# First softmax rows taken ahead of the visits in a fused attention and feed-forward kernel

## The chip, the cores and the metric

The kernel runs on one core of one Trainium2 chip. The metric is the device time of one execution in microseconds; the median of the runs is compared. Besides that time there is one profiled execution with a trace of every instruction. The engines are called PE (matrix products), PEld (its weight loads), DVE (VectorE), ACT (ScalarE), POOL (GpSimd) and SP (which issues most of the DMAs).

## The reference

Two blocks follow each other. The first is an attention with 32 inducing rows, in two steps; the second a feed-forward layer with a leaky activation whose slope `alpha` belongs to each hidden unit.

```python
# x: (4, 12480, 128), inducing: (32, 128)
def mab(q, kv):
    s = scale * (q @ kv.transpose(0, 2, 1))
    s = s - s.max(-1, keepdims=True)
    a = np.exp(s)
    a /= a.sum(-1, keepdims=True) + 1e-09
    return a @ kv
h = mab(I, x)          # 32 rows look at all rows of a batch
y = mab(x, h)          # every row looks at the 32 rows
# the feed-forward layer: d_model 128, d_ff 2048
u = y @ w_in
g = np.maximum(u, 0.0) + alpha * np.minimum(u, 0.0)
out = g @ w_out
```

Inputs and output are float32; the kernel multiplies in bfloat16.

## The kernel before

The rows of a batch are cut into six super-tiles of 16 tiles of 128 rows, and a short rest of one and a half tiles; the rests of the four batches are done together at the end. The kernel first works through the whole first attention step of batch 0 (the start). Then come the visits. One visit takes a block of four tiles (512 rows) and four of the 16 slices of the hidden units: PE makes four products `hh` of 32x512 operands (line 808, in `visit`), each into a PSUM bank of its own; DVE or ACT applies the relu and writes `gt` (lines 823 and 821); in the visit after, PE makes 16 products of `gt` and the weights `W1` (line 834, in `second`) that are summed in the block's bank `bp`. So a block takes four visits, a super-tile 16, and the whole 390. PSUM has eight banks, and they are shared by everything.

The value `y` is never made: `HW` is the product of the 32 rows `h` and `w_in`, so the softmax weights of a row, turned into the operand `a2`, give `hh` directly. The leaky part is linear: with `Amat`, the product of `w_in` and the alpha-weighted `w_out` (`linear_product`, line 996), `a_lin` makes `HA` (lines 619 and 621), and `linear` adds it for two blocks at a time (line 861). For the first pair of blocks this is put off to visit 8, where `finish` for the first block is put off too.

The softmax weights of a super-tile take several steps: scores on PE (`b_products`, line 644) and their copy (`b_scores`, line 702 or 704), maximum (line 721, DVE), subtraction (line 726, POOL), exponential (line 688, ACT), sum (line 712, POOL), reciprocal (`b_rec`, line 749, DVE), multiplication (line 757, POOL) and the turn by a transposing DMA (`b_turn`, line 766). For the first super-tile this takes too long, so it has a way of its own: maximum, subtraction and exponential without copy (lines 675, 679 and 773), the turn of tiles 0 to 7 by PE and a copy (lines 779 and 787), that of tiles 8 to 15 by a POOL copy and a DMA (`first_turn_dma`, lines 1144 and 1147); the division by the sum comes at the end of the block, by the reciprocal `rec` (`first_sum`, line 1154 on POOL; `first_rec`, line 1167 on DVE; used in line 880). The scores of tiles 4 to 15 wait in the eighth bank (`later`).

The order of the instructions is written out by hand. In the start it is the string `order`, whose words are carried out by `begin`; `W5` is five products without use. In the visits every step is put at a visit with `at(n, step, ..., cost=...)`; it is issued at the end of that visit, behind the visit's own relus on each engine. A table `when` holds the visits of the eight steps of a super-tile. A planner (`Plan.choose`) looks at all visits with assumed costs ahead of time and chooses, by a beam search, which engine does each relu and copy, which bank is used, and whether a step runs at once or in the middle of the visit after. It begins with a state: when PE, ACT and DVE are free, and when each bank is. Steps on POOL and DMAs have no cost in it.

```python
start = tuple(self.NEVER if k == BANKS - 1 else 0.0 for k in range(BANKS))
beam = [((0.0, 0.0, 0.0, (0.0,) * R, start, (), ()), None)]
```

The end of `order`, and the steps of the ramp that follow it:

```python
W4 b bm b2 bs be w hwv W5 bt ba W5
...
at(6, first_rec, cost=[("v", 160)])
at(6, linear_product, cost=[("s", 900), ("v", 210), ("!", 0)])
at(7, a_lin, st, cost=[("s", 260), ("v", 210)])
```

Of the kernel before, what the change touches and what calls it, by code (L numbers as in the profile page):

```python
# [21 lines left out]
P = 128  # L22
R = 4
ST = 16
BT = 4
# [5 lines left out]
def kernel(  # L31
# [80 lines left out]
    class Plan:  # L112
# [115 lines left out]
            return (*new, tuple(held.items()), tuple(waits)), used  # L228

        def choose(self):  # L230
            start = tuple(self.NEVER if k == BANKS - 1 else 0.0 for k in range(BANKS))
            beam = [((0.0, 0.0, 0.0, (0.0,) * R, start, (), ()), None)]
            relus = ["".join(w) for w in product("av", repeat=R) if 0 < w.count("a") < R]
            for n, (*_, chains) in enumerate(self.visits):
                ways = []
                for chain in chains:
                    kinds = [k for k, _ in chain]
                    if "f" in kinds:
                        ways.append([e + w for e in "av" for w in "nl"])
                    elif "!" in kinds or not {"a", "v"} & set(kinds):  # L240
                        ways.append([""])
                    else:
                        ways.append(["n", "l"])
                found = {}
                for state, path in beam:
                    for way in product(*ways):
                        for relu in relus:
                            new, used = self.step(state, n, relu, way)
                            at = new[0] + 390
                            over = max(new[1] - at, 0) + max(new[2] - at, 0)  # L250
                            over += sum(w[1] for w in new[6]) * 0.3
                            score = new[0] + 0.3 * over
                            ends = sorted(max(x - new[0], -200) for x in new[4])
                            key = (
                                *(int(x - new[0]) // 16 for x in new[1:3] + new[3]),
                                *(int(x) // 16 for x in ends if x < self.NEVER / 2),
                                new[6],
                            )
                            if key not in found or score < found[key][0]:
                                found[key] = (score, new, (path, relu + "".join(way), used))  # L260
                best = sorted(found.values(), key=lambda f: f[0])[: self.WIDTH]
                beam = [(new, path) for _, new, path in best]
            path, taken, banks = beam[0][1], [], []
            while path:
                path, these, used = path
                taken.append(these)
                banks.append(used)
            self.taken = iter("".join(reversed(taken)))
            self.banks = iter([k for used in reversed(banks) for k in used])
# [405 lines left out]
        nc.vector.tensor_reduce(out=m[:, :n], in_=ps[:, t0 : t0 + n, :], axis=AX, op=MAX)  # L675
        return m

    def b_less(ps, t0, n, m, e):
        nc.vector.tensor_tensor(
            out=e[:, :n],  # L680
            in0=ps[:, t0 : t0 + n, :],
            in1=m[:, :n].unsqueeze(2).broadcast_to([P, n, M]),
            op=SUB,
        )

# [6 lines left out]
    def new_e():  # L692
        return e2_pool.tile([P, ST, M], f32, name="e2", tag="e2")
# [77 lines left out]
    def b_exp_once(e, n, w):  # L771

        nc.scalar.activation(out=w, in_=e[:, :n], func=EXP, scale=scale)
# [235 lines left out]
    def first_most():  # L1009
        kept["bm"] = b_most(kept["b"], 0, BT)  # L1010

    def first_less():
        kept["be"] = new_e()
        b_less(kept["b"], 0, BT, kept["bm"], kept["be"])
# [23 lines left out]
    def begin(step):  # L1038


        if step[0] == "W":
            warm(int(step[1:]))
            return
        plain = {
            "mg": lambda: a_max(st),
            "rb": lambda: kept.update(rb=a_factors_pe(st)),
            "mm": lambda: a_factors_min(st, kept["rb"]),
            "mf": lambda: a_factors_exp(st),
            "ex": lambda: a_worth(st),
            "dn": lambda: a_total(st),  # L1050
            "pd": lambda: kept.update(pd=a_den_pe(st)),
            "rec": lambda: a_den_rec(st, kept["pd"]),
            "ph": lambda: kept.update(ph=a_sum_pe(st)),
            "hT": lambda: a_sum_div(st, kept["ph"]),
            "b": first_products,
            "bm": first_most,
            "bs": first_less,
            "be": lambda: b_exp_once(kept["be"], BT, w0[:, :BT]),
            "bt": lambda: kept.update(bt=b_turn_pe(w0[:, :BT], BT)),
            "ba": lambda: b_turn_copy(st, 0, 0, BT, kept["bt"], False),  # L1060
            "b2": lambda: b_products(st, 0, BT, ST - BT, later),
            "w": lambda: a_w(st),
            "al": lambda: kept.update(al=alpha_turn()),
            "alc": lambda: nc.vector.tensor_copy(out=alT[:], in_=kept["al"][:]),
            "kwp": lambda: nc.gpsimd.tensor_copy(out=w_in_b[:], in_=kept["w_in"][:]),
            "om": lambda: nc.gpsimd.tensor_scalar(
                out=om_al[:], in0=alT[:], scalar1=-1.0, scalar2=1.0, op0=MULT, op1=ADD
            ),
            "hw": lambda: a_w_copy(st),
            "hwv": lambda: a_w_copy(st, False),  # L1070
        }
        if step in plain:
            plain[step]()
            return
        f, act = step[0], step[-1] == "a"
        p, _, part = step[1:].rstrip("avp").partition(".")
        pc = first_pieces[int(p)]
        if f in "tc":
            t0, n = cuts[pc.n][int(part)]
            if f == "t":  # L1080
                kept["t", p, part] = a_turn_pe(st, pc, t0, n)
            else:
                a_turn_copy(st, pc, t0, n, kept.pop(("t", p, part)), act)
        elif f == "k":
            a_cast_part(st, pc, *cuts[pc.n][int(part)], step[-1])
            done = first_pieces[int(p)].s
            if pc.full and step == last_cast[done]:
                load_next(done)
            if step == weights_after:
                load_weights()  # L1090
        elif f == "u":
            kept["u", p] = a_e1_pe(st, pc)
        elif f == "v":
            a_e1_copy(st, pc, kept.pop(("u", p)), act)
        else:
            {"s": a_scores, "m": a_least, "e": a_exp, "f": a_fac, "h": a_h, "g": a_add}[f](st, pc)
# [13 lines left out]
        c5.1a e4 k7.0p f4 om kwp t6.1 c5.2v c5.0v W2 t6.0 c6.1v s5 t7.1 u3 c6.0v t7.0 m5  # L1110
        c7.0v s6 u4 f3 c7.1a m6 v3a W1 h3 e5 v4v e6 s7 f5 m7 W2 u5 mg f6 h4 v5v g3 u6 e7
        ex f7 g4 W1 h5 rb v6v u7 g5 v7a h6 mm mf dn g6 W2 h7 g7 pd rec W1 ph hT W4 b bm
        b2 bs be w hwv W5 bt ba W5
    """
    waiting = [first_pieces[5:6], first_pieces[6:]]
    last_cast = {}
# [4 lines left out]
    for step in order.split():  # L1121
        begin(step)
        if step == "kwp":
# [2 lines left out]
                weights(i, nc.gpsimd)  # L1126
            for i in range(NV):
                linear_weights(i)
    e2s = {}

    def first_rest_less(t0, n):
        e2s[t0] = new_e()
        b_less(later, t0, n, b_most(later, t0, n), e2s[t0])

    def first_rest_exp(t0, n):
        b_exp_once(e2s[t0], n, w0[:, t0 : t0 + n])

    def first_turn():
        act = plan.on_act()
# [59 lines left out]

        todo.setdefault(max(n, 0), []).append((fn, args, cost))  # L1200

    at(0, first_rest_less, BT, BT, cost=[("v", 600), ("!", 0)])
    at(1, first_rest_exp, BT, BT, cost=[("a", 330), ("!", 0)])
    at(1, first_rest_less, H, H, cost=[("v", 780), ("free", BANKS - 1), ("!", 0)])
    at(2, first_turn, cost=[("s", 350), ("f", 0)])
    at(2, first_rest_exp, H, H, cost=[("a", 560), ("!", 0)])
    at(2, first_turn_dma)
    at(6, first_rec, cost=[("v", 160)])
    at(6, linear_product, cost=[("s", 900), ("v", 210), ("!", 0)])
    at(7, a_lin, st, cost=[("s", 260), ("v", 210)])  # L1210
    blocks[0].later = True

    def on(b, fn, *args):
# [2 lines left out]
    for b, s, nt in groups[1:]:  # L1216
        n = first[b, s]
        when = [n - 23, n - 19, n - 16, n - 14, n - 13, n - 11, n - 9, n - 6]
        if (b, s) == (0, 1):
            when = [1, 2, 3, 4, 5, 7, 8, 8]  # L1220
        if (b, s) == (0, 2):
            when[7] = n - 7
        at(when[0], on, b, b_scores, s, nt, cost=[("s", 25 * nt), ("f", 0)])
        at(when[1], on, b, b_max, s, nt, cost=[("v", 70 + 33 * nt)])
        at(when[2], on, b, b_less_pool, s, nt)
        at(
            when[3],
            lambda b=b, s=s, nt=nt: b_exp(states[b].e2[s], nt),
            cost=[("a", 100 + 27 * nt)],
        )  # L1230
        at(when[4], on, b, b_sum, s, nt)
        at(when[5], on, b, b_rec, s, nt, cost=[("v", 160)])
        at(when[6], on, b, b_mul, s, nt)
        at(when[7], on, b, b_turn, s, 0, nt)
# [130 lines left out]
```

## Time and profile before

| | |
|---|---|
| median of 3 runs | 594.98 us (593.67 to 595.17) |
| the profiled execution | 593.7 us |
| its span in the trace | 591.9 us |
| mean granted clock of TensorE | 0.998 |
| start, up to the first `hh` of visit 0 | 30.03 us |
| instructions | 23144 |

The span runs from the first to the last instruction of the trace; some 1.8 us of the execution lie outside it. All times of single instructions below are counted from the start of the span. A row of the timeline gives start, length, engine, line, operation, what is written and read, how many instructions were merged, and in brackets the idle time of the engine before it and what ended it. In the chain of waits a row is a start, a length and what the chain went through.

### The profile page before, as it was taken

What the parts mean: (1) busy time and instruction counts of PE and PEld (TensorE: products, weight loads), DVE (VectorE), ACT (ScalarE), POOL (GpSimd) and SP (SyncE); (2) the same over time, 40 slices, a digit from 0 to 9 for tenths busy, and PEclk for the clock granted to TensorE, in tenths of its full rate; (3) what the DMA queues carried; (4) which work ended last, traced back from release to release, by engine and by line L of the source; (5) the groups of instructions that cost most, each with busy time, mean ns of one, the idle gap of its engine ahead of it and who ended that gap; (6) DMA issues with size and microseconds to landing.
All of it is one profiled execution on the core that took longest, in us unless ns stands there. A gap on an engine that the chain in (4) does not pass through costs nothing.

```text
span 591.9 us, 23144 instructions
## 1 busy us (share of the span) xinstructions
PE 584.5 (99%) x9500; PEld 441.3 (75%) x9500; DVE 535.5 (90%) x978; ACT 537.3 (91%) x1086; POOL 216.6 (37%) x260
## 2 busy tenths in 40 slices
PE   9999999999999999999999999999999999999997
PEld 6667777777777777777777777777777777777776
DVE  5889999999999898999999899999999999989996
ACT  5698999999999999999999999999999998999986
POOL 3494633323326426313226256124034034144010
PEclk9999999999999999999999999999999999999999
DMA  8969999233187999631368999731321331532421
GB/s 338 265 180 167 250 207 225 62 90 91 38 237 161 209 193 211 127 82 60 86 151 180 190 249 207 144 100 38 92 72 55 92 75 53 119 81 61 91 69 47
DMA packets 122347, 80.56 MB, mean 136 GB/s; under 512 B 103760, under 2 KB 106112, under 8 KB 119168
## 3 DMA queue, kind: packets, MB, share of 16 engines
q1 hardware_dynamic: 122016, 78.99, 56.3%
q8 instruction: 74, 1.21, 0.9%
q14 instruction: 33, 0.27, 0.2%
q10 hardware_dynamic: 224, 0.09, 0.1%
HBM read 28.07 MB, written 25.56 MB: 91 GB/s over the span
## 4 chain that ended last, share of the span: by engine, by line
PE 91%; DMA 5%; POOL 2%; DVE 0%; issue 0%; DVEq 0%; SPq 0%; ACT 0%; POOLq 0%
PE bp L834 64%; PE hh L808 21%; DMA xs<-in_x_dram 3%; PE bp L861 2%; DMA w_out_f<-in_moe_w_out_dram 2%; PE hh L644 2%; PE hh L473 1%; PE hh L379 1%; DMA e<-e1T 1%; POOL W L977 1%; POOL AW L986 1%; POOL t L712 0%; DVE gt L823 0%; DVEq L1360 0%; DVE xn L349 0%
## 5 line engine op out<-in xcount | busy, mean ns | idle before, releaser
L821 ACT ACTIVATE gt<-hh 128x512 bf16<-128x512 f32 x854 | 454.8, 605 | 36.0 <-PE hh L808 30.9
L823 DVE TENSOR_SCALAR gt<-hh 128x512 bf16<-128x512 f32 x706 | 453.5, 684 | 23.8 <-PE hh L808 13.3
L834 PE MATMUL bp<-W,gt 128*128 128x128 bf16 x6240 | 417.3, 220 | 0.2 <-DVE gt L823 0.2
L834 PEld LDWEIGHTS <-gt 128*128 128x128 bf16 x6240 | 349.4, 98 | 84.9 <-issue 76.6
L808 PE MATMUL hh<-a,HW 32*128 32x512 bf16 (+2 forms) x1664 | 156.2, 371 | 0.5 <-ACT gt L821 0.5
L757 POOL TENSOR_TENSOR rep<-e,rc 128x2048 bf16<-128x2048 f32 (+1 forms) x24 | 84.5, 3520 | 23.9 <-DVE rc L749 23.5
L726 POOL TENSOR_TENSOR e<-e,smx 128x512 f32<-128x512 f32 (+1 forms) x24 | 24.6, 1025 | 156.4 <-ACT gt L821 89.6
L808 PEld LDWEIGHTS <-HW 32*128 32x128 bf16 x1664 | 40.6, 91 | 41.7 <-issue 5.6
L712 POOL TENSOR_TENSOR t<-e 128x256 f32<-128x256 f32 (+1 forms) x24 | 17.2, 717 | 139.8 <-ACT e L688 139.7
L887 ACT COPY ob<-bp 128x512 f32<-128x512 f32 (+1 forms) x62 | 36.3, 585 | 4.3 <-PE bp L834 1.4
L712 POOL TENSOR_TENSOR t<-t 128x128 f32<-128x128 f32 (+3 forms) x100 | 30.3, 303 | 7.8
L330 POOL CAST xn<-xs 128x2048 bf16<-128x2048 f32 x17 | 32.1, 1888 | 2.8 <-DMA xs<-in_x_dram 2.3
L889 DVE COPY ob<-bp 128x512 f32<-128x512 f32 x32 | 22.0, 687 | 6.0 <-PE bp L834 6.0
L861 PEld LDWEIGHTS <-a 32*128 32x128 bf16 x392 | 15.0, 93 | 6.3 <-issue 0.5
L393 DVE TENSOR_SCALAR_CACHE_REDUCE s<-hh 128x512 f32<-128x512 f32 (+2 forms) x29 | 18.0, 619 | 1.6 <-PE hh L379 1.6
L861 PE MATMUL bp<-HA,a 32*128 32x128 bf16 x392 | 19.1, 214 | 0.2 <-DVE HA L621 0.2
L418 ACT ACTIVATE e1T<-s,rm 128x512 bf16<-128x512 f32 (+1 forms) x25 | 17.9, 718 | 0.6 <-DVE rm L402 0.6
L721 DVE TENSOR_REDUCE smx<-e 128x16 f32<-128x512 f32 (+1 forms) x24 | 15.9, 662 | 0.0
L963 PE MATMUL bp<-blank 128*128 128x256 bf16 x78 | 14.0, 316 | 1.2 <-DVE blank L909 1.2
L688 ACT ACTIVATE e<-e 128x512 f32<-128x512 f32 (+1 forms) x24 | 15.0, 625 | 0.2 <-POOL e L726 0.2
L489 DVE SCALAR_TENSOR_TENSOR hs<-hs,fac,hh 128x128 f32<-128x128 f32 (+1 forms) x25 | 8.6, 344 | 6.4 <-PE hh L473 5.7
L702 ACT COPY e<-hh 128x512 f32<-128x512 f32 (+1 forms) x23 | 13.9, 606 | 0.2
(110 smaller groups left out, 203.7 us busy)
## 6 DMA issues: line engine op xcount, KB each, us to landing
out_dram<-ob SPq DMA_DIRECT2D x97, 256.0 KB, 2.7
xs<-in_x_dram SPq DMA_DIRECT2D x23, 1024.0 KB, 6.6
xs<-in_x_dram SPq DMA_DIRECT2D x2, 512.0 KB, 9.1
w_in_f<-in_moe_w_in_dram SPq DMA_DIRECT2D x1, 1024.0 KB, 4.8
a<-rep SPq DMA_TRANSPOSE x25, 4.7
xT<-xn SPq DMA_TRANSPOSE x18, 6.0
e<-e1T SPq DMA_TRANSPOSE x18, 3.8
xs_left<-in_x_dram SPq DMA_DIRECT2D x4, 64.0 KB, 5.2
```

Source lines behind the costliest of these rows:

```text
L330: nc.gpsimd.tensor_copy(out=st.xn[s][:], in_=xs[:])
L393: nc.vector.tensor_scalar(out=s1[:parts, :cols], in0=ps[:parts, :cols], scalar1=-scale, scalar2=None, op0=MULT, op1=MIN, accum_out=st.mx[: ...
L712: nc.gpsimd.tensor_tensor(out=t[:, :n], in0=src[:, :n, :w], in1=src[:, :n, w : 2 * w], op=ADD)
L726: nc.gpsimd.tensor_tensor(out=st.e2[s][:, :n], in0=st.e2[s][:, :n], in1=st.m2[s][:, :n].unsqueeze(2).broadcast_to([P, n, M]), op=SUB,)
L757: nc.gpsimd.tensor_tensor(out=rep[:, :n], in0=st.e2[s][:, :n].unsqueeze(2).broadcast_to([P, n, R, M]), in1=rc[:, :n].unsqueeze(2).unsqueez ...
L808: nc.tensor.matmul(hh[:, q * cols + w.start : q * cols + w.stop], HWs[b][rows, v * P : (v + 1) * P], a2[rows, t0 : t0 + nt, :].rearrange(" ...
L821: nc.scalar.activation(out=gt[:, :cols], in_=hh[:, :cols], func=RELU)
L823: nc.vector.tensor_relu(gt[:, :cols], hh[:, :cols])
L834: nc.tensor.matmul(blk.acc[:, t * C : (t + 1) * C], gt[:, (q * nt + t) * P : (q * nt + t + 1) * P], W1[:, k, :], start=(not blk.begun), st ...
L861: nc.tensor.matmul(blk.acc[w, t * C : (t + 1) * C], blk.a2[rows, blk.t0 + t, w], HAs[b][rows, :], start=(not blk.begun and t == 0), stop=F ...
L887: nc.scalar.copy(out=ob[:, :nt], in_=acc)
L889: nc.vector.tensor_copy(out=ob[:, :nt], in_=acc)
```

## The change

The maximum of tiles 4 to 15 of the first super-tile is taken in one instruction ahead of the visits (`rx`), and so are the subtractions of tiles 4 to 7 (`rl`) and 8 to 15 (`rk`) and the exponential of tiles 4 to 7 (`re`). The cast of `HW` in the start goes from DVE (`hwv`) to ACT (`hw`). The turn of tiles 4 to 7 (`first_turn`) goes from visit 2 to visit 0, and the scores of the second super-tile from visit 1 to visit 0. In the ramp `linear_product` goes from visit 6 to 5, `a_lin` from 7 to 6, and the reciprocal of the second super-tile (`b_rec`) from 7 to 8. The planner begins with the eighth bank free at 430 ns and DVE free at 330 ns.

```diff
-            start = tuple(self.NEVER if k == BANKS - 1 else 0.0 for k in range(BANKS))
-            beam = [((0.0, 0.0, 0.0, (0.0,) * R, start, (), ()), None)]
+            start = tuple(430.0 if k == BANKS - 1 else 0.0 for k in range(BANKS))
+            beam = [((0.0, 0.0, 330.0, (0.0,) * R, start, (), ()), None)]
...
-    def b_less(ps, t0, n, m, e):
+    def b_less(ps, t0, n, m, e, a=0):
         nc.vector.tensor_tensor(
-            out=e[:, :n],
+            out=e[:, a : a + n],
             in0=ps[:, t0 : t0 + n, :],
-            in1=m[:, :n].unsqueeze(2).broadcast_to([P, n, M]),
+            in1=m[:, a : a + n].unsqueeze(2).broadcast_to([P, n, M]),
             op=SUB,
         )
...
+    def rest_most():
+        kept["rm"] = b_most(later, BT, ST - BT)
+        kept["re"] = new_e()
+
+    def rest_less(t0, n):
+        b_less(later, t0, n, kept["rm"], kept["re"], t0 - BT)
+
+    def rest_exp(t0, n):
+        b_exp_once(kept["re"][:, t0 - BT :], n, w0[:, t0 : t0 + n])
...
+            "rx": rest_most,
+            "rl": lambda: rest_less(BT, BT),
+            "rk": lambda: rest_less(H, H),
+            "re": lambda: rest_exp(BT, BT),
...
-        b2 bs be w hwv W5 bt ba W5
+        b2 bs be w rx hw rl W5 re bt ba rk W5
...
-    at(0, first_rest_less, BT, BT, cost=[("v", 600), ("!", 0)])
-    at(1, first_rest_exp, BT, BT, cost=[("a", 330), ("!", 0)])
-    at(1, first_rest_less, H, H, cost=[("v", 780), ("free", BANKS - 1), ("!", 0)])
-    at(2, first_turn, cost=[("s", 350), ("f", 0)])
-    at(2, first_rest_exp, H, H, cost=[("a", 560), ("!", 0)])
+    at(2, rest_exp, H, H, cost=[("a", 560), ("!", 0)])
+    at(0, first_turn, cost=[("s", 350), ("f", 0)])
     at(2, first_turn_dma)
     at(6, first_rec, cost=[("v", 160)])
-    at(6, linear_product, cost=[("s", 900), ("v", 210), ("!", 0)])
-    at(7, a_lin, st, cost=[("s", 260), ("v", 210)])
+    at(5, linear_product, cost=[("s", 900), ("v", 210), ("!", 0)])
+    at(6, a_lin, st, cost=[("s", 260), ("v", 210)])
...
         if (b, s) == (0, 1):
-            when = [1, 2, 3, 4, 5, 7, 8, 8]
+            when = [0, 2, 3, 4, 5, 8, 8, 8]
```

More of the change, by code (lines that the diff above doesn't have):

```diff
@@ L1128 @@
                 linear_weights(i)
[L1129 to L1136, printed above, removed]
     def first_turn():
```

## The prediction

> **What bounds the kernel now.** I read four views, in this order: the page, the chain of waits over the first 60 us, the timeline of the ramp (24 to 54 us), and the starts of single visits in that timeline. On the page TensorE is the engine that never rests:
>
> ```profile
> PE 584.5 (99%) x9500; PEld 441.3 (75%) x9500; DVE 535.5 (90%) x978; ACT 537.3 (91%) x1086; POOL 216.6 (37%) x260
> ```
>
> So time can be won only where PE waits. The chain of waits says where that is: after the loads and the weights it runs through POOL and DVE until 43.2 us, and from there on it is PE's own work.
>
> ```profile
> 33.07 3.99 POOL AW L986 x4
> ...
> 41.16 0.22 POOL den L1154
> 41.38 0.02 issue
> 41.40 0.04 DVE rec L1167
> 41.44 0.13 issue
> 41.57 0.23 DVE Amat L999
> 41.80 1.19 DVE gt L823 x2
> 42.99 0.21 DVE HA L621
> ```
>
> The timeline shows the starts of the visits (the four L808 matmuls) and what stands between them. A plain visit in the steady part takes 1.33 us:
>
> ```profile
> 50.79 0.40 PE L808 MATMUL hh<-a,HW 32*128 32x512 bf16 x4
> 52.12 0.39 PE L808 MATMUL hh<-a,HW 32*128 32x512 bf16 x4
> ```
>
> The ramp, before and after visit 0 starts at 30.03:
>
> ```profile
> 28.51 0.69 DVE L607 CAST HW<-hh 128x512 bf16<-128x512 f32 x1
> 28.51 0.31 ACT L773 ACTIVATE rep<-e 128x128 bf16<-128x128 f32 x1 [2.39 <-DVE e L679]
> 29.49 0.42 DVE L787 COPY a<-hh 128x512 bf16<-128x512 bf16 x1 [0.30 <-PE hh L779]
> ...
> 30.03 0.61 PE L808 MATMUL hh<-a,HW 32*128 32x512 bf16 x7
> 31.13 0.37 PE L808 MATMUL hh<-a,HW 32*128 32x512 bf16 x1 [0.49 <-ACT gt L821]
> 31.43 0.91 PEld L834 LDWEIGHTS <-gt 128*128 128x128 bf16 x16 [1.19 <-DVE smx L675]
> 32.78 0.41 DVE L675 TENSOR_REDUCE smx<-bp 128x8 f32<-128x256 f32 x1
> 33.29 0.42 DVE L679 TENSOR_TENSOR e<-bp,smx 128x256 f32<-128x256 f32 x1
> ```
>
> Three idle stretches of PE follow.
> Fill: visit 0 starts at 30.03, visit 4 at 35.87, so 5.84. The work in it is four times 0.33 (L808) plus three times 1.00 (L834, one visit behind), plus 0.39 for the scores of the second super-tile and 0.39 for the turn (a visit with scores runs from 91.60 to 93.32, one with a turn from 32.83 to 34.55, both 1.72 against 1.33): 5.10. Idle 0.74. The eighth L808 waits at 31.13 for a PSUM bank, and L834 behind it for the first relu outputs and an eighth and ninth bank.
> Visit 8: 42.24 to 44.57 is 2.33; another visit with the L861 products, 49.24 to 50.79, is 1.55. Idle 0.78: L861 waits for HA (42.91 to 43.19), which on DVE stands behind two relus, Amat and the reciprocal L1167, which waits for POOL's L1154 (ready 41.38).
> Visit 9: 44.57 to 46.59 is 2.02, against 1.72 with scores. Idle 0.30: the fourth L808 waits for a bank, because DVE stood 0.86 in front of
>
> ```profile
> 44.05 0.25 DVE L749 RECIPROCAL rc<-den 128x16 f32<-128x16 f32 x1 [0.86 <-POOL den L736]
> ```
>
> In all 1.82 us. After that little is left: in the PE rows 278 plain visits are never under 1.325 and add up to only 2.6 us above that, ramp excluded, in crumbs.
>
> **Part by part.** *Ahead of the visits, DVE.* It gains one maximum over 12 tiles and two subtractions (128x128, 128x256), and loses the HW cast. From L675 at 0.28 (128 columns) and 0.41 (256) the maximum of 384 columns is about 0.54 (an estimate; ends 0.41 and 0.69, those two rows alone and together). From 28.51: maximum to 29.05, subtraction of 0.29 to about 29.45, and L787 cannot start before 29.49 anyway, because PE's transposes end then. So visit 0 stays at 30.03; at the upper end it comes 0.1 late, and nothing makes it earlier. The last subtraction (0.42) runs 29.92 to 30.35, while the first relu could not start before 30.45. Cover: 0.1 us; if gone, the first DVE relu slips by that much.
> *ACT.* HW cast after the first exp, from 28.83. L605, the same cast of the later batches on ACT, takes 0.592; DVE's took 0.692. HW is ready at 29.42, 0.6 before it is used. The exp of four tiles (0.34) follows and ends at 29.8, before its turn is issued at 30.36. Cost nothing, under ACT's idle 1.66 before 30.48. [...]
> *Removed from visits 0 to 2:* on DVE 0.28+0.29+0.41+0.42 = 1.40, on ACT 0.34. No moved step issues a DMA; POOL's order and SP's queue keep theirs.
> *Scores and turn in visit 0.* After four L808 (30.36) PE does the turn and the scores, 0.78, to 31.14: work that fills the wait instead of following it. Banks: four for visit 0, one for each of the two, four for visit 1, one for the sum: eleven of eight, k7 included from 30.4 on. The first two relus end at 31.08 to 31.13, just as visit 1 needs its third bank; the next two at 31.6 to 31.75, so L834 starts at about 31.70. Two copies (0.42 turn, 0.6 scores) now stand among the relus and cost visit 2 about 0.1 on its fourth bank. Then 31.70+1.00+0.33+0.10+1.00+0.33+1.00 puts visit 4 at 35.46 instead of 35.87: gain 0.41. Ends: 0.74 (no idle), and a loss of 0.3 if both copies stand ahead of visit 1's relus on one engine.
> *Amat product in visit 5, HA in visit 6.* The L996 product (0.90 of PE) needs AW, done at 37.07; visit 5's turn for it comes at about 38.0. Amat is then off the reciprocal's back. HA stays behind L1167, which still waits until 41.40; queued behind that on DVE are HA and visit 7's relus, and PE waits for both. HA ends at about 41.85, visit 7's two DVE relus at 43.1, visit 8 starts at 41.83. Its L861 would run at 42.05, its L834 to 43.45 at the earliest; short banks (visit 7's not yet free) make that 43.8. Against 44.57: 0.77, so 0.36 beyond the fill. Ends 0.78 and 0.
> *Second reciprocal from visit 7 to 8.* DVE no longer stands 0.86 in front of L749; it passes it after both L880. Visit 9's 0.30 goes to about 0.15: gain 0.15, ends 0.30 and 0. What is late next: the multiplication on POOL behind it (rival below).
> *Three numbers of the planner* cost no time themselves, but all 390 visits are planned anew. The 2.6 us of crumbs may go up or down; I take 0 with 0.8 either way.
> Sum: 0.41+0.36+0.15 = 0.92 us won (ends 1.82 won, 0.3 lost). The profiled execution took 593.7 with a span of 591.9; it should come to 592.8. The median shown is 594.98, 1.28 above it: 594.1.
>
> **Rivals.**
> A, the whole idle time goes (1.82), perhaps with fewer crumbs: 593.2 down to 592.6. For it: the relu engines are relieved of 1.74 us exactly there. Against it: L1154 on POOL does not move, and DVE reaches it earlier than before. So does ACT its exp L688, which cannot start before 38.95; it idled 0.24 there and would idle some 0.8.
> B, slower: visit 16 waits for its operand. From L749 at 44.05 the operand needs 0.39, 3.61 on POOL, and 4.3 from DMA issue (48.07) to landing: 52.4, i.e. L749 plus 8.35. Visit 16 began at 54.77 and would now at 53.9. With L749 behind two L880 and a relu I expect it at 45.1 to 45.9, landing at 53.5 to 54.3: just on time. From 45.5 on every delay is paid; past 46.4 the gain is gone; at 47.5, behind two more relus, the kernel comes to 596.1, at 48.2 to 596.8.
> C, slower: the planner charges nothing for POOL, so it hands relus of visits 5 to 8 to an engine that in fact stands before POOL. Four badly placed relus at 0.6 to 0.7 with crumbs grown: 596.5 to 597.
> [...]
>
> **The numbers.** A measurement of this kernel tells 0.3%, 1.8 us, from no change: under 593.2 counts as faster, over 596.8 as slower. My forecast, 594.1 (own range 593.3 to 595.2, the ends of the sum with part of the crumbs): 0.50. A: 0.27. B: 0.11, C: 0.09, D: 0.03. I count B and C whole as slower, since their far ends lie there, and D as no change. Faster 0.27, same 0.53, slower 0.20. The range runs from A's lower end, 592.6, to 596.6, near the far end of B and inside C, leaving out some 0.2.
>
> **What would show it.** In the profile after: visit 0 still at 30.0; L779's second group and L644 between the first and the second four L808; L834 first at about 31.7, with no idle over 0.3; visit 4 near 35.5; L996 before visit 6; L1167 still at 41.4, with DVE idle before it; L861 of visit 8 by 42.7; visit 9 near 43.8; L749 at 45 to 46, and no wait of PE at visit 16. The forecast is wrong if visit 0 moves, if visit 9 starts after 44.4, if visit 16 waits for the DMA, or if plain visits average over 1.34.

## The result and the profile after

The changed kernel is slower: 596.56 us median (595.12 to 598.6, 12 runs) against 593.70 (592.79 to 595.17, 12 runs), a ratio of 1.0047 (95% interval 1.0035 to 1.0059). The profiled execution took 597.49, its span is 595.6, 3.7 more than before's. The time lies just inside the range; the sign was forecast wrongly, and more than half of the chances went to no change. That the time lies inside is luck: the forecast was counted from a median of three runs, 594.98, which the twelve runs put at 593.70, and the top end of the range came from two rivals.

The page: PE works 1.3 us longer than before (584.5), and the span has grown by more.

```profile
PE 585.8 (98%) x9500; PEld 442.1 (74%) x9500; DVE 535.9 (90%) x978; ACT 537.4 (90%) x1085; POOL 216.7 (36%) x260
```

The ramp in the timeline after; these rows answer to those shown of before:

```profile
28.75 0.57 ACT L605 CAST HW<-hh 128x512 bf16<-128x512 f32 x1
29.52 0.42 DVE L787 COPY a<-hh 128x512 bf16<-128x512 bf16 x1 [0.23 <-PE hh L779]
29.86 0.41 DVE L679 TENSOR_TENSOR e<-bp,smx 128x256 f32<-128x256 f32 x1
30.05 0.40 PE L808 MATMUL hh<-a,HW 32*128 32x512 bf16 x4
30.38 0.41 PE L779 MATMUL hh<-ident,rep 128*32 128x128 bf16 x16
30.72 0.56 PE L644 MATMUL hh<-hT,xT 128*128 128x32 bf16 x16
31.61 0.90 PEld L834 LDWEIGHTS <-gt 128*128 128x128 bf16 x16 [0.30 <-ACT gt L821]
...
40.62 0.28 DVE L621 CAST HA<-hh 128x128 bf16<-128x128 f32 x1
40.98 0.25 DVE L1173 RECIPROCAL rec<-den 128x16 f32<-128x16 f32 x1
44.05 0.39 PE L808 MATMUL hh<-a,HW 32*128 32x512 bf16 x4
44.20 0.24 DVE L749 RECIPROCAL rc<-den 128x16 f32<-128x16 f32 x1
44.36 1.22 DVE L880 TENSOR_TENSOR ob<-bp,rec 128x512 f32<-128x512 f32 x2
44.58 3.61 POOL L757 TENSOR_TENSOR rep<-e,rc 128x2048 bf16<-128x2048 f32 x1 [0.99 <-PE hh L808]
```

The ramp did what it was to do: visit 0 at 30.05, turn and scores in the gap, visit 9 at 44.05. Counting the first L808 of each visit, visit 10 starts 0.82 us earlier than before, and this lead stays the same to 0.01 us until visit 31. There it ends. The chain of waits now has, at 74 us, a DMA that before's chain does not have, and the waits of PE and the timeline name it:

```profile
74.25 6.42 DMA a<-rep
```

```profile
PE hh L808 <- DMA a<-rep: 3.1, 1, 3.1
```

```profile
80.72 0.50 PE L808 MATMUL hh<-a,HW 32*128 32x512 bf16 x4 [3.09 <-DMA a<-rep]
```

Before, the same visit starts without a wait:

```profile
78.39 0.40 PE L808 MATMUL hh<-a,HW 32*128 32x512 bf16 x4
```

Visit 32 is the first of the third super-tile; its operand is turned by the DMA of L766. From visit 31 to 32 it takes 4.48 instead of 1.33. The restart costs 0.92 more in visit 32 and 0.31 up to visit 36; DVE and ACT had been idle for 3.1 and 3.0 us when it began, and from 80.9 to 84.3 the granted clock of TensorE was 0.50, against 1.00 just before and after: the 16 L834 of visit 32 took 1.89 there, 1.07 in a plain visit. From there the distance hardly moves. So the account of the spans is -0.82 (ramp) + 3.15 + 0.92 + 0.31 + 0.14 (all visits after 36) = 3.7.

Why the turn came late is seen in part on SP's queue, here before and after:

```profile
48.07 1.78 SPq L766 DMA_TRANSPOSE a<-rep  x1
49.95 1.56 SPq L894 DMA_DIRECT2D out_dram<-ob  x2
51.61 1.17 SPq L356 DMA_TRANSPOSE xT<-xn_left  x1
52.88 3.13 SPq L356 DMA_TRANSPOSE xT<-xn  x1
56.06 0.57 SPq L315 DMA_DIRECT2D xs<-in_x_dram  x1
...
66.28 3.00 SPq L356 DMA_TRANSPOSE xT<-xn  x1
...
72.93 2.31 SPq L766 DMA_TRANSPOSE a<-rep  x1
```

```profile
48.22 1.78 SPq L766 DMA_TRANSPOSE a<-rep  x1
50.10 1.57 SPq L894 DMA_DIRECT2D out_dram<-ob  x2
51.76 2.37 SPq L356 DMA_TRANSPOSE xT<-xn_left  x1
54.22 3.26 SPq L356 DMA_TRANSPOSE xT<-xn  x1
57.53 0.97 SPq L315 DMA_DIRECT2D xs<-in_x_dram  x1
...
66.53 4.00 SPq L356 DMA_TRANSPOSE xT<-xn  x1
...
74.25 3.11 SPq L766 DMA_TRANSPOSE a<-rep  x1
```

The second super-tile's turn (the first row) is issued 0.15 later, although PE is 0.82 ahead. Then the first two outputs, issued from 50.1 on, take 5.1 and 4.6 us to land instead of 3.0 and 2.7. The issue of L356 behind them holds the queue for 2.37 instead of 1.17, and the next two rows slip by 1.3 and 1.5. Some issues at 62 to 64 us are early again, with PE; but POOL's cast waits 1.96 for the load `xs`, the turn of L356 behind it holds the queue for 4.00 instead of 3.00, and from 70 us on all are 1.3 late.

```profile
64.61 1.89 POOL L330 CAST xn<-xs 128x2048 bf16<-128x2048 f32 x1 [1.96 <-DMA xs<-in_x_dram]
```

The third turn is issued at 74.25, 1.32 later, takes 6.42 instead of 5.37 and lands at 80.68. Before, it landed at 78.30, and visit 32 began at 78.39: there was 0.09 us to spare, and a lead of PE that the turn does not share would have been lost there.

The stretches view of 53.5 to 56 us (columns: busy time of PE, PEld, DVE, ACT and POOL with counts, clock, DMA share of 16 engines, GB/s), first after, then before, shows that the DMA engines then did almost nothing, with outputs and turns outstanding:

```profile
53.50:56.00 2.50, 2.50 (x41) 1.84 (x39) 2.46 (x5) 2.02 (x5) 0.00 (x0) 1.00 0.18 32
```

```profile
53.50:56.00 2.50, 2.50 (x41) 1.93 (x40) 2.43 (x5) 2.10 (x5) 0.47 (x1) 1.00 1.01 74
```

Among the trace's packets are loads of the program itself, in the queues that the page calls "instruction": 16 KB (q8) and 8 KB (q14) each. In the changed kernel one of q8 began at 51.99 and took 1.76, one of q14 at 53.62 and took 2.23, amid the outputs; before they began at 53.48 and 54.08, when the outputs had all but landed, and took 1.14 and 0.63. The DMA view of 49 to 56 us has one of each, their time as a share of 16 engines; first after, then before:

```profile
q14 instruction: 1, 0.01, 2.0%
q8 instruction: 1, 0.02, 1.6%
```

```profile
q8 instruction: 1, 0.02, 1.0%
q14 instruction: 1, 0.01, 0.6%
```

### The profile page after: what moved, and what is told of

Same layout as the page of the kernel before. It is cut to its first block, busy times and chain, and to the rows that moved or that the text cites. A ratio compares the mean times of both kernels' runs of the same rounds, so it can differ in the third digit from the quotient of the medians.

```text
span 595.6 us, 23148 instructions
## 1 busy us (share of the span) xinstructions
PE 585.8 (98%) x9500; PEld 442.1 (74%) x9500; DVE 535.9 (90%) x978; ACT 537.4 (90%) x1085; POOL 216.7 (36%) x260
## 4 chain that ended last, share of the span: by engine, by line
PE 94%; DMA 4%; DVE 1%; ACT 0%; issue 0%; DVEq 0%; POOL 0%; SPq 0%
PE bp L834 64%; PE hh L808 21%; DMA xs<-in_x_dram 3%; PE bp L861 2%; PE hh L644 2%; PE hh L473 1%; DMA a<-rep 1%; PE hh L379 1%; DVE gt L823 1%; PE bp L963 1%; PE hh L364 0%; PE hh L598 0%; PE hh L456 0%; DVEq L1363 0%; DVE xn L349 0%
## 5 line engine op out<-in xcount | busy, mean ns | idle before, releaser
L834 PE MATMUL bp<-W,gt 128*128 128x128 bf16 x6240 | 418.1, 220 | 0.2 <-DVE gt L823 0.2
L834 PEld LDWEIGHTS <-gt 128*128 128x128 bf16 x6240 | 350.4, 98 | 84.7 <-issue 77.2
L808 PE MATMUL hh<-a,HW 32*128 32x512 bf16 (+2 forms) x1664 | 156.8, 371 | 3.2 <-DMA a<-rep 3.1
L757 POOL TENSOR_TENSOR rep<-e,rc 128x2048 bf16<-128x2048 f32 (+1 forms) x24 | 84.5, 3521 | 24.4 <-DVE rc L749 23.4
L808 PEld LDWEIGHTS <-HW 32*128 32x128 bf16 x1664 | 40.5, 91 | 45.2 <-issue 6.3
```

The lines of the kernel that those rows point to most:

```text
L757: nc.gpsimd.tensor_tensor(out=rep[:, :n], in0=st.e2[s][:, :n].unsqueeze(2).broadcast_to([P, n, R, M]), in1=rc[:, :n].unsqueeze(2).unsqueez ...
L808: nc.tensor.matmul(hh[:, q * cols + w.start : q * cols + w.stop], HWs[b][rows, v * P : (v + 1) * P], a2[rows, t0 : t0 + nt, :].rearrange(" ...
L834: nc.tensor.matmul(blk.acc[:, t * C : (t + 1) * C], gt[:, (q * nt + t) * P : (q * nt + t + 1) * P], W1[:, k, :], start=(not blk.begun), st ...
```

## The experiments

My theory after this was in two parts. "Landing": the lead is real, but it ran into a transfer that had no time to spare. "Program loads": the extra lateness comes from loads of PE's program that the change put among the first outputs. The rivals were the reciprocal's new place, and a worse plan for all visits. The kernels before and after are called B and A. Each ratio is to runs of B made beside that kernel; their medians go from 593.18 to 593.74, so two kernels are compared by their ratios. All distances below are the starts of the first L808 in the traces.

**a_rec7**: A with the reciprocal back at its place.

```diff
-            when = [0, 2, 3, 4, 5, 8, 8, 8]
+            when = [0, 2, 3, 4, 5, 7, 8, 8]
```

> The changed kernel with the reciprocal of the second super-tile back at visit 7. Theory 'landing': PE's lead of 0.82 us is real, but the operand of the third super-tile (visit 32) landed only 0.1 us before its use in the kernel before, and SP's queue behind the second super-tile's turn did not get earlier; then an earlier reciprocal (43.7 instead of 44.2) moves that turn and all behind it up by 0.5, PE loses 0.3 of its lead, and a wait of 1.5 to 2.5 stays at visit 32: 595 to 596. Rival 'reciprocal': the move to visit 8 alone made the operand late; then the wait at visit 32 is gone and the time is 592.9 to 593.3. Rival 'program loads' (transfers at 50 us collide with PE's program loads): wait as in the changed kernel, about 3, 596.5.

593.79, ratio 1.0007 (0.9995 to 1.0019). Nothing waits at visit 32: the operand lands at 77.68, visit 32 starts at 78.07. Both parts of my theory had forecast a wait here, of 1.5 to 2.5 and of about 3, and were wrong in that. But visit 10 is 16.09 after visit 0 instead of 15.72. So the move to visit 8 is worth 0.4 in the ramp, over twice the 0.15 that I gave it, and is at the same time what leads to the loss: it holds back the second turn (47.68 here, 48.22 in A), while it lets PE run ahead. So the rival "reciprocal" is half right; why the landing moves by 3.0 us it does not say.

**a_turn23** and **b_turn23**: the third turn two visits earlier on SP's queue, in A and in B.

```diff
         if (b, s) == (0, 2):
-            when[7] = n - 7
+            when[7] = n - 9
```

> The changed kernel with the turn of the third super-tile issued at visit 23 instead of 25, that is ahead of one other transposing DMA and an output on SP's queue. 'Landing' and 'program loads' alike: issued at about 71.9 instead of 74.25, landing near 78.2, wait at visit 32 0.9 or less, time 594 to 594.4. If the loss were spread over the new plan's visits instead: no change, 596.5.

594.18, 1.0010 (1.0001 to 1.0020): by the ratios 2.2 us better than A. The turn lands at 75.95 and visit 32 does not wait. Some of it comes back between visits 36 and 50, 2.2 us in the trace, with new waits for DMAs:

```profile
PE hh L473 <- DMA e<-e1T: 1.3, 1, 1.3
...
PE hh L808 <- DMA a<-rep: 0.8, 1, 0.8
```

The outputs were slow here as well (3.5 and 5.4); that the queue stayed late for this reason, and the next in it paid, is a reading that no run isolates. A worse plan for the visits is not the cause of A's loss.

> The kernel before with the same move of the turn from visit 25 to 23. 'Landing': nothing waited there, so no gain: within 0.3 us of the kernel before, and the operand lands some 2 us ahead of visit 32. If the kernel before lost time there in runs that were not profiled: faster by up to 0.5.

593.72, 1.0005 (0.9995 to 1.0014), as expected no gain: the operand lands at 74.81, three us ahead, and nobody needs that in B.

**a_phase** and **b_shift24**: more PE instructions at the very start, in the same PE time, so that the loads of PE's program fall elsewhere. In A the load at 52.0 goes away from the outputs, in B the load at 53.5 goes onto them. The helper `warm` gets a second argument, the number of columns.

```diff
-    warm(17)
+    warm(51, 85)    # a_phase, both places; b_shift24: warm(29, 150)
```

> The changed kernel with the two opening blocks of 17 products of 256 columns without use made into 51 of 85 columns each: about the same PE time, but 136 more PE instructions ahead of everything, half of the distance between two loads of PE's program, so that these loads fall at other places. 'Program loads': the first outputs take about 3 us instead of 5.1, the operand lands near 78.3, the wait at visit 32 falls to about 0.8, time 593.8 to 594.4. 'Landing' without any part of the program loads: unchanged, wait 3, 596.5.

593.45, 1.0001 (0.9992 to 1.0009): by the ratios 2.7 us better than A, with an edit that touches no visit. The load comes at 47.87, the next at 57.09; the outputs take 2.6 and 2.5; the third turn is issued at 71.37, the operand lands at 77.67, and of the wait 0.2 is left:

```profile
PE hh L808 <- DMA a<-rep: 0.2, 1, 0.2
```

> The kernel before, with the two opening blocks of 17 products without use as 29 of 150 columns each: the same PE time, 48 more PE instructions, so that the load of PE's program that fell at 53.5 us falls at about 51.9, onto the first outputs, as in the changed kernel; nothing else is changed. 'Program loads': the first outputs take 4.5 us or more instead of 3.0, the operand of the third super-tile lands at 79.5 to 80.7, PE waits 1 to 2.3 at visit 32, time 594.5 to 596. 'Landing' without program loads (the changed kernel's own order makes the transfers late): no change, 593.4.

594.19, 1.0014 (1.0003 to 1.0025): 0.8 slower than B by the ratio, less than expected. The load comes at 51.32, 2.1 after the first output's issue; the outputs take 4.5 and 4.9, the operand lands at 79.09, earlier than expected, and B has A's wait:

```profile
PE hh L808 <- DMA a<-rep: 1.4, 1, 1.4
```

So the place of the program loads makes transfers late or lets them land in time, both ways shown: the first output took 5.13 in A and 2.6 in a_phase, 2.96 in B and 4.5 in b_shift24. But the way from there to visit 32 is not one and the same. In b_shift24 the slow outputs did not make the queue late: the third turn was issued 42.76 after visit 0, against 42.90 in B. It took 6.51 to land instead of 5.37, and another load of PE's program began at 76.70, while it was under way. A has such a load too, at 77.26, and this is the other part of its lateness (1.05, beside 1.32 at the issue); a_phase has one at 73.44 (6.30), and its gain is all in the issue. My theory had only the loads among the outputs. That slow outputs make the queue late is supported by a_phase, where both go away together, and not by b_shift24.

In the traces of A, of B and of their parts, without a shift, the outputs are fast or slow mostly by where PE's load falls behind the first output's issue. A star marks a load of PE's program that began between the third turn's issue and its landing:

| kernel | load after the issue, us | first two outputs took | third turn took | landed | visit 32 began |
|---|---|---|---|---|---|
| B | 3.53 | 2.96, 2.66 | 5.37 | 78.30 | 78.39 |
| a_fill (below) | 3.86 | 2.97, 2.69 | 5.29 | 77.90 | 78.22 |
| a_lin67 (below) | 3.63 | 2.96, 4.31 | 5.33 | 78.62 | 78.79 |
| b_turn23 | 3.51 | 2.96, 2.67 | 4.67 | 74.81 | 77.86 |
| a_rec7 | 3.39 | 2.92, 4.27 | 5.05 | 77.68 | 78.07 |
| before_again (below) | 3.29 | 2.92, 4.20 | 5.37 | 77.39 | 77.72 |
| a_turn23 | 2.97 | 3.48, 5.42 | 5.75* | 75.95 | 76.97 |
| A | 1.89 | 5.13, 4.60 | 6.42* | 80.68 | 80.72 |
| b_places (below) | 1.82 | 4.83, 4.31 | 6.28* | 80.55 | 80.60 |

With the load at 2 us after the issue both outputs are slow; at 3.3 to 3.9 the first is fast, and the second, issued some 1.2 later, either way. In all 15 traces the third turn took 5.75 to 6.51 where a load began within it, and 4.67 to 5.37 elsewhere. The loads follow PE: 136 more of its instructions moved the one at 51.99 to 47.87. The outputs follow POOL and SP: in A L757 ends at 48.19, the second turn is issued at 48.22 and the first output behind it at 50.10. A lead of PE and a delay of the second turn both shift the one against the other; the change made both, 0.82 and 0.15.

**before_again, a_lin67, a_fill, b_places**: what the lead consists of. `before_again` is B once more. `a_lin67` puts the Amat product and HA back to visits 6 and 7; `a_fill` the reciprocal too, so that only the softmax part is left; `b_places` is B with these three places alone.

```diff
+    at(6, linear_product, ...)     # a_lin67, a_fill; b_places: 5
+    at(7, a_lin, st, ...)          # a_lin67, a_fill; b_places: 6
+            when = [0, 2, 3, 4, 5, 7, 8, 8]   # a_fill; b_places: [1, 2, 3, 4, 5, 8, 8, 8]
```

> The kernel before, unchanged, for a second trace. If the start of POOL's weight products (29.04 in the first trace, when w_out landed at 28.90; 28.6 in the changed kernel's) sets L1154 and with it visits 8 and 9, visit 10 comes up to 0.5 earlier where w_out lands at 28.4, and the lead of the changed kernel is 0.3, not 0.82. If visit 10 is at 46.6 again with an earlier landing, the lead is the change's own.

> The changed kernel with the Amat product back at visit 6 and HA at 7; only the ramp is read. By the sum of the prediction this gives back 0.36 of the lead by visit 10, more if DVE's wait for L1154 stands in front of Amat again (up to 0.8). If only POOL's L1154 counts: no change by visit 10.

> The changed kernel with the Amat product back at visit 6, HA at 7 and the reciprocal at 7: only the softmax steps, the turn and the scores are moved. By the prediction's sum visit 4 stays 0.4 to 0.6 earlier after visit 0 than in the kernel before (5.85) and visit 10 too (16.1 there with w_out at 28.4). If POOL's L1154 holds visits 8 to 10 whatever came before: visit 4 at 5.25, visit 10 at 16.1 or later, no gain.

> The kernel before with the three places alone (Amat product at 5, HA at 6, reciprocal at 8). By the sum: visit 4 as before (5.85), visit 10 0.4 to 0.5 earlier, 15.6. If the places help only where the ramp is ahead already: 16.0.

One trace each, so the visits are compared, not the times (592.76, 594.57, 593.49, 595.61). All in us after visit 0, with the end of `den`, POOL's first sum of softmax weights (L1154, or its line in the other kernels), which follows the landing of w_out; the last column is the distance from `den` to visit 10:

| kernel | den | visit 4 | visit 10 | visit 10 after den |
|---|---|---|---|---|
| B, first trace | 11.34 | 5.85 | 16.57 | 5.22 |
| before_again | 11.05 | 5.85 | 16.27 | 5.22 |
| b_turn23 | 10.81 | 5.85 | 16.02 | 5.22 |
| a_lin67 | 10.89 | 5.26 | 16.92 | 6.03 |
| a_rec7 | 10.88 | 5.21 | 16.09 | 5.22 |
| b_places | 10.86 | 5.85 | 15.68 | 4.82 |
| A | 10.89 | 5.21 | 15.72 | 4.83 |
| a_fill | 9.83 | 5.25 | 15.86 | 6.03 |
| b_phase_turn23 (below) | 9.61 | 5.85 | 15.80 | 6.19 |
| a_phase_turn23 (below) | 9.87 | 5.21 | 14.91 | 5.05 |

Three things follow. While `den` ends 10.8 or more after visit 0, visit 10 keeps a fixed distance to it, 5.22 in B and 4.83 in A, and my trace of B had a late one (w_out landed at 28.90; in the others of B at 27.6 to 28.4): with equal `den` the lead is 0.39 and not 0.82. The softmax part wins 0.6 by visit 4 and has lost it again by visit 10: `b_places` without it is as early as A, and `a_rec7`, with it and with Amat and HA, is level with B. And a part alone can do harm: `a_lin67` comes 0.8 later behind `den` than B and gives back 1.2 of A's lead, more than the 0.8 that I had as the most; `a_fill` has the same 6.03, though its `den` is early. `b_places` also has A's wait at visit 32 (80.60), so that the three places, not the softmax part, brought it.

**a_phase_turn23, b_phase_turn23, a_split_phase_turn23, b_split_phase_turn23**: A and B without a wait at visit 32 (both edits above), and with w_out loaded in four parts, so that POOL can begin on the first.

```diff
-        nc.sync.dma_start(out=kept["w_out"][:], in_=...)
+        for i in range(NV):
+            ks = slice(i * R, (i + 1) * R)
+            nc.sync.dma_start(out=kept["w_out"][:, ks, :], in_=...[:, ks, :])
```

> The changed kernel with shifted program loads (51 of 85) and with the third super-tile's turn at visit 23. Both theories: operand lands near 75, no wait at visit 32. If the lead of the ramp is a gain of the change itself: 0.7 to 0.9 under the kernel before, 592.5 to 592.7. If most of the lead came from an earlier landing of w_out in the profiled run: 593.0 to 593.3.

> The kernel before with the shifted program loads and the third turn at visit 23, so that neither kernel waits at visit 32; beside the changed kernel treated alike (593.0, ratio 0.9996 to the kernel before) this gives the change's own worth. If the ramp's lead is the change's: 0.4 to 0.7 slower than that one, 593.4 to 593.7. If new plan and DMA luck are all: the same, 593.0.

Both came to a ratio of 0.9996, with intervals of 0.9985 to 1.0006 and 0.9987 to 1.0005 (593.00 and 593.53; each had runs of B of its own, of 593.18 and 593.74): with the wait gone, A and B can't be told apart. In the two traces `den` happened to be early, and there A is 0.9 ahead at visit 10.

> The changed kernel with shifted program loads, the third turn at visit 23, and w_out loaded by four DMAs of 256 KB instead of one of 1 MB, so that POOL's weight products start on the first quarter. If POOL's chain is what holds visits 6 to 10 and the transfers behind them: L977 starts near 25.5 instead of 28.5, L1154 ends 1 to 3 us earlier, visit 10 comes at 14.9 after visit 0 or before, no wait at visit 32, time 591.8 to 592.6, under both kernels. If the products still wait for the last quarter: as without the split, 593.0.

> The kernel before with w_out in four DMAs, shifted program loads and the third turn at visit 23. If the change is worth something once POOL's chain is early: visit 10 at about 15.8 after visit 0 (14.9 in the changed kernel treated alike), ratio to the kernel before near 0.9990 against 0.9977, some 0.8 us slower than the changed kernel treated alike. If the split alone makes the gain: 14.9 and 0.9977 as well.

592.61 against 593.74 for B in its own form, ratio 0.9977 (0.9967 to 0.9988): the one version that beats both kernels. B with the same three edits: 1.0003 (0.9992 to 1.0015), where 0.9990 was expected. The timeline of POOL in the faster one:

```profile
25.38 4.04 POOL L977 TENSOR_TENSOR W<-w_out_f,om_al 128x512 bf16<-128x512 f32 x4
...
35.46 0.82 POOL L1153 COPY rep<-rep 128x768 bf16<-128x768 bf16 x1 [1.97 <-ACT rep L773]
...
40.31 0.21 POOL L1163 TENSOR_SCALAR den<-t 128x16 f32<-128x16 f32 x1
```

The weight products begin 3.2 us earlier than in A. POOL then waits for the exponential at 35.46, no longer the other way round; `den` ends 9.86 after visit 0 and visit 10 starts at 14.91, in B with the same edits at 15.80 (46.78 less 30.98). So once POOL's chain is not the last to end, the change is worth 0.9 us in the ramp, and 1.5 us by the two ratios (1.1 by the medians). Which part of the change makes the 0.9 no run isolates.

The split has a price in the start: in its two traces visit 0 begins at 30.66 (A) and 30.98 (B), later than in the other 13 (29.55 to 30.57), and PE waits ahead of it for DVE, here in the kernel B with the three edits:

```profile
PE hh L567 <- DVE den L554: 0.6, 1, 0.6
```

In A with the three edits this wait is 0.3, so 0.3 of the distance between the two traces lies ahead of the visits. What makes DVE late there was not tested.

## Why the prediction was right or wrong

- *Visit 0 does not move; ACT's cast is free*: right. L605 took 0.57 on ACT, against 0.69 of DVE's. No run shows a cast on ACT so slow that visit 0 comes late, which the 0.03 for D stood on: visit 0 started at 30.05 against 30.03.
- *Fill*: right at visit 4, where 0.41 was forecast and 0.61 measured (L834 at 31.61 against 31.70). The two copies cost visit 2 nothing: visits 2 to 5 are 1.33 apart. But the sum carried this gain on to visit 10, and there nothing of it is left (`b_places` against A, `a_rec7` against B).
- *Amat and HA*: 0.36 forecast beyond the fill. The step failed in its premises that L1167 stays at 41.4 and that HA stands behind it. The reciprocal (L1173 in A) ran at 40.98, since POOL started 0.45 earlier for another reason, the landing of w_out, and HA ran ahead of it, at 40.62. I took a chance value of one trace for a fixed date. With equal `den`, fill and this together are worth nothing by visit 10 (`a_rec7`, 5.22 as in B) instead of 0.77.
- *Second reciprocal*: 0.15 forecast, about 0.4 measured (a_rec7). Its time was forecast at 45.1 to 45.9, behind both L880; it ran ahead of them at 44.20, so the operand of visit 16 came in time (52.51 against 53.95), and rival B did not occur at its place.
- *The sum of the ramp*: 0.92 forecast, 0.82 in the traces; that these are so close is luck, since some 0.45 of it is not the change's. The other part, 0.39, is less than half, and the three terms do not add up one by one.
- *The planner's crumbs*: within my 0.8; visits 36 to 380 take 488.95 against 488.79. Rival C did not occur.
- *What failed*: the step that let the ramp's gain go through to the end ("After that little is left"). I asked only PE's rows whether visits wait, and looked at the operand's way only as far as visit 16. The same view for the next super-tile shows an operand landing 0.09 us before its use. Since "no moved step issues a DMA" I took SP's queue as unchanged. Its order was; its time did not move with PE, and loads of PE's program met its transfers at other points: the third turn was issued 1.32 later, took 1.05 longer, and PE waited 3.09 for it. Rival B's mechanism was the right one (an operand turned by DMA that comes late for a PE running ahead), its place visit 32 and its price 3.2 and a restart of 1.2, and it had a chance of 0.11.

## What to carry to other kernels

A gain at the start of a long kernel can be lost at a later transfer that has less time to spare and does not move with it; here a lead of 0.82 us met one with 0.09 to spare. So list, for each operand that comes by DMA, its landing and its first use, and look first at the smallest difference. Compare a second trace of the same kernel before a wait of some tenths is explained or removed; here half of a lead was the landing of one load. Where two chains run on different engines, moving one ahead can also change which transfers meet: with PE 0.82 ahead and the second turn 0.15 behind, a load of PE's program came 1.89 after the first output's issue instead of 3.53.

## What the runs showed of the hardware

Transfers of data took longer where a load of PE's program fell among them. The loads of PE's program, 16 KB each, came 7.9 us apart on average in A (3.6 to 15.4); 136 more PE instructions at the start moved the one at 51.99 to 47.87. Where such a load began within 2.1 us behind the issue of one of the first two outputs, its 256 KB took 4.1 to 5.4 us; where it began 2.6 us or more behind, or had ended before, 2.4 to 3.5; in between it was either. The turns of L766 show the same. Over the 15 traces, without the short last turn of each, 86 turns with no load of PE's program under way between issue and landing took 4.28 to 5.37 us, 4.48 on average, and 259 with one took 4.27 to 6.90, 5.35 on average; in the trace of A and the first of B alone 12 without took 4.50 on average and 34 with one 5.39. With 48 PE instructions without use B became 0.8 us slower by the ratio.

That the loads of q8 are PE's is read from the traces: 74 of them, 16 KB each, for the 19000 instructions of PE and PEld on the page, 257 to a load, and the shift of 4.1 us by the 136 instructions. The loads of q14 have 8 KB. PE itself did not wait for instructions in a way that the traces show, but the data transfers took longer. What held the last part of the outputs back after 53.5 us in A, at a DMA share of 0.18 and 32 GB/s, is not shown by any run.
